# Loading V as rows of two neighbouring keys, between columns of ones

## The chip, the cores and the metric

The kernel runs on one core of one Trainium2 chip. TensorE multiplies matrices, VectorE, ScalarE and GpSimd compute elementwise, and 16 DMA engines move data; SyncE only issues transfers. The metric is the device time of one execution in microseconds (us); the number given for a kernel is the median of several executions. A profile is taken of one execution more, and it has its own time.

## The reference

The reference is one block of a conditioned transformer: an attention part with cached keys and values, then a mixer with two small matrix products and a feed-forward pair. Cut to the attention, where the change lies:

```
q = (h @ wq) as 32 heads of 128 columns            # h: [2048, 640], layer norm of x, modulated by c
scores = q @ k_cache.T * 128 ** -0.5               # per head [2048 queries, 2048 keys]
p = softmax(scores)
o = p @ v_cache                                    # v_cache: [32 heads, 2048 keys, 128], bf16
x = x + ga * (o of all heads, side by side, @ wo)
```

The sum over keys in the softmax's denominator and in `p @ v` does not depend on the order in which the keys are taken, as long as both factors of the product use the same one.

## The kernel before

**Steps and tiles.** The attention is one loop of 512 steps and some more at its end. Step `s` starts tile `s`: 128 queries of head `s // 16`, so that a head has 16 tiles. In one step, in the order in which each engine gets its work:

- TensorE makes the scores of tile `s` in two halves of 1024 keys into PSUM (`qk`, L294 with the helper L15), and behind each half the eight products of half a tile that is 8 steps older with V (`pv`, L307; `PVD = 8`). In most steps there is also one piece of the next head's queries (`q_piece`, L245) or of a transpose (`t_piece`, L261) behind each half.
- VectorE takes each half of the scores out of PSUM, multiplies by minus the scale, and keeps the smallest value of each row (L584). The result, `negS`, has three buffers.
- GpSimd takes the smaller of the two minima (L594, `nm`), and ScalarE makes the exponentials of the 2048 scores of each query with it as bias (L597): in `negS` float32, out `Pb` bf16, queries on the partitions, keys along the row.
- `pv` needs the exponentials with keys on the partitions. 14 of the 16 tiles of a head are transposed by DMA (`transpose`, L230), most of them two tiles at a time; tiles 3 and 10 of each head are transposed on TensorE (L261, copied out by L270 and L272). The transposed tile `PTs` has 16 blocks of 128 keys, which are the stationary operands of the 16 products of `pv`.
- ScalarE copies the finished outputs of two tiles out of PSUM (`Of`, L575). GpSimd makes the reciprocals of four tiles' sums at a time (`rcp`, L448, a power of minus one), multiplies each tile by it (`norm`, L455), and sends four tiles to a scratch array in HBM (L462).

**V and the sums.** `load_v` (L222) fills one of two buffers of `Vaug`: for each of the 16 blocks of 128 keys, partition `p` gets the 128 values of key `128 t + p`, that is one row of 256 B, and behind them lie two columns of ones that are written once (L350). Each product of `pv` reads 129 columns, 128 of V and a one, so that column 128 of the output is the sum of the exponentials.

**Order of the transfers.** All loads and all DMA transposes are issued by SyncE in one queue, in the order in which the program lists them; an issue that has to wait holds up those behind it. Counted by the tile `j` of a head's own steps, the queue has for each head: the transpose of tiles (0, 1), that of tile 2, the keys of the next head (L213, `j = 2`, itself a transposing load), tiles (4, 5), the weights of the queries of the head after next (L217, `j = 6`), tiles (6, 7), (8, 9), V of the next head (L222, `j = 9`), tile 11, tiles (12, 13), and (14, 15). A step's waits are worked out by a small planner (`Prog._add`): each operation names what it reads and writes, and gets a semaphore wait for every unfinished writer or reader of these.

**After the loop** the scratch array is read back transposed, multiplied by `wo`, and the mixer and the feed-forward part run (L532 to L846). The change does not touch these, but for the size of `Of`.

## Time and profile before

| | |
|---|---|
| median of 3 executions | 1593.01 us (1591.46 to 1596.07) |
| the profiled execution | 1592.4 us, of which the span from the first to the last instruction is 1590.6 us |
| granted TensorE clock, mean | 0.996 |
| VectorE, L584, half a tile of scores | 1024 of 1220 ns |
| ScalarE, L597, exponentials of a tile | 512 of 2018 ns |
| TensorE, L307, products with V | 8192 of 220 ns each from start to modelled end; they overlap |
| GpSimd, L448, reciprocals of four tiles | 128 of 1040 ns |
| DMA transposes of exponentials (L230) | 256, median 7.0 us from issue to landing |
| loads of V (L222) | 32 of 512 KB, median 5.0 us from issue to landing |

How to read it: each engine works through its own list, and an instruction that waits holds up the ones behind it. The profile gives, for each group of instructions of a source line, the busy time and the idle time of the engine just before them, with what ended that idle time. The rows of SPq are SyncE's own instructions. Instructions of one engine overlap by some tens of nanoseconds, so the step from one start to the next is shorter than a duration: L584 takes 1.22 us and follows itself after 1.145 us (641.26 and 642.41 us are two successive starts), L597 takes 2.0 us and holds ScalarE for 1.90 us (611.49 to 613.40 us, starts of two with nothing between). The loop takes the time from about 39 us to about 1280 us.

### The profile page before, as it was taken

Reading aid. Unit: us, or ns where it says so; the run is one execution under the profiler, and the core shown is the slowest. Engines: PE = TensorE matmul, PEld = TensorE weight load, DVE = VectorE, ACT = ScalarE, POOL = GpSimd, SP = SyncE. Lnnn points to the kernel's source line nnn. Section 1 sums busy time; section 2 is a strip of 40 time slices with the busy share of each in tenths; the row PEclk is TensorE's granted clock in tenths of the full one; section 3 lists DMA queues with packets and bytes.
Section 4 is the critical chain, followed back from the end, with each engine's and each line's share of the span. In section 5 each row is a group of like instructions: output and inputs, shape, how many; then the busy total and the mean of one; then the engine's idle time right before and its main releaser. Section 6 shows DMA issues by size and latency. Waiting matters only on the chain.

```text
span 1590.6 us, 33595 instructions
## 1 busy us (share of the span) xinstructions
PE 1477.4 (93%) x13976; PEld 916.9 (58%) x13207; DVE 1395.0 (88%) x2463; ACT 1295.8 (81%) x1145; POOL 622.0 (39%) x1396
## 2 busy tenths in 40 slices
PE   5899999999999999999999999999999889999999
PEld 3466655656565556665556565565656655555555
DVE  6999999999999999999999999999999646666435
ACT  4999999999999999999999999999999700036330
POOL 0244444444444444444444444444444523223100
PEclk9999999999999999999999999999999999999999
DMA  9999999999999999999999999999999997503000
GB/s 300 236 235 237 240 236 239 242 233 251 235 245 236 233 242 241 239 244 228 245 238 236 236 248 230 243 242 237 243 230 236 240 248 135 127 1 112 9 26 34
DMA packets 1167900, 333.53 MB, mean 210 GB/s; under 512 B 1148352, under 2 KB 1161728, under 8 KB 1167744
## 3 DMA queue, kind: packets, MB, share of 16 engines
q1 hardware_dynamic: 1161600, 314.59, 98.5%
q0 software_dynamic: 6144, 16.79, 3.7%
q8 instruction: 108, 1.77, 0.5%
q14 instruction: 48, 0.39, 0.1%
HBM read 43.48 MB, written 19.40 MB: 40 GB/s over the span
## 4 chain that ended last, share of the span: by engine, by line
DVE 34%; ACT 22%; PE 21%; DMA 13%; issue 9%; POOL 2%; SPq 0%; POOLq 0%; DVEq 0%
DVE negS L584 31%; ACT ring L597 18%; DMA ring<-ring 12%; PE Sps L532 8%; PE Sps L836 4%; ACT ring L270 2%; PE Oaug L787 2%; PE QPp L787 2%; PE Sps L772 1%; ACT kv L252 1%; ACT Of L575 1%; PE PTp L307 1%; DVE ring L272 1%; DMA negS<-o_scratch 1%; POOL small L594 1%
## 5 line engine op out<-in xcount | busy, mean ns | idle before, releaser
L584 DVE TENSOR_SCALAR_CACHE_REDUCE negS<-Sps 128x1024 f32<-128x1024 f32 x1024 | 1178.6, 1220 | 30.9 <-PE Sps L15 30.5
L597 ACT ACTIVATE ring<-negS,small 128x2048 bf16<-128x2048 f32 x512 | 1029.6, 2018 | 22.8 <-POOL small L594 20.7
L307 PEld LDWEIGHTS PTp<-kv,ring 128*128 128x128 bf16 x8192 | 550.7, 98 | 382.7 <-issue 112.9
L307 PE MATMUL PTp<-kv,ring 128*128 128x129 bf16 x8192 | 645.7, 220 | 49.0 <-DMA ring<-ring 48.6
L15 PE MATMUL Sps<-kv 128*128 128x512 bf16 x1024 | 387.9, 379 | 12.6 <-DVE negS L584 6.6
L594 POOL TENSOR_SCALAR small<-small 128x1 f32<-128x1 f32 x512 | 145.8, 285 | 631.5 <-DVE negS L584 631.5
L294 PE MATMUL Sps<-kv 128*128 128x512 bf16 x926 | 355.3, 384 | 21.9 <-DVE negS L584 10.8
L455 POOL TENSOR_SCALAR On<-Of,small 128x128 bf16<-128x128 f32 x512 | 190.0, 371 | 13.0
L294 PEld LDWEIGHTS Sps<-kv 128*128 128x128 bf16 x1024 | 98.3, 96 | 109.3 <-DVE negS L584 87.2
L448 POOL TENSOR_TENSOR small<-Of,small 128x4 f32<-128x4 f32 x128 | 133.1, 1040 | 9.2 <-ACT Of L575 9.2
L675 ACT COPY kv<-PTp 128x640 bf16<-128x640 bf16 x32 | 22.0, 692 | 127.7 <-PE PTp L672 127.6
L462 POOL DMA_DIRECT2D o_scratch<-On x128 | 103.1, 806 | 40.8 <-POOL On L455 37.2
L575 ACT COPY Of<-PTp 128x259 f32<-128x259 f32 x256 | 96.0, 375 | 14.3 <-PE PTp L307 14.3
L245 PE MATMUL Oaug<-hTx,kv 128*128 128x512 bf16 x264 | 100.4, 385 | 3.4 <-DVE hTx L404 3.4
L245 PE MATMUL QPp<-hTx,kv 128*128 128x512 bf16 x259 | 97.5, 381 | 2.4 <-ACT hTx L399 1.7
L584 DVE DVE_READ_ACCUMULATOR negS<-Sps 128x1 f32 x1024 | 84.9, 83 | 0.0
L631 POOL TENSOR_SCALAR negS<-negS 128x1 f32<-128x1 f32 x48 | 24.7, 514 | 138.5 <-DVE negS L640 138.3
L532 PE MATMUL Sps<-wo,negS 128*128 128x128 bf16 (+1 forms) x503 | 71.4, 300 | 4.5 <-DMA negS<-o_scratch 4.1
L532 PE MATMUL Sps<-wo,hTx 128*128 128x512 bf16 (+1 forms) x502 | 69.3, 297 | 0.5
L645 DVE TENSOR_TENSOR ring<-Sps,mod_bc 128x640 f32<-128x640 f32 x16 | 13.2, 825 | 62.1 <-PE Sps L532 40.7
L270 ACT COPY ring<-Oaug 128x1024 bf16<-128x1024 bf16 x64 | 65.4, 1022 | 0.0
L840 DVE TENSOR_TENSOR ring<-Sps,ring 128x640 f32<-128x640 f32 x15 | 12.4, 824 | 58.5 <-PE Sps L836 58.5
(91 smaller groups left out, 1043.4 us busy)
## 6 DMA issues: line engine op xcount, KB each, us to landing
kv<-in_A_v_cache_dram SPq DMA_DIRECT2D x32, 512.0 KB, 5.0
o_scratch<-On POOLq DMA_DIRECT2D x128, 128.0 KB, 3.8
kv<-in_A_wq_dram SPq DMA_DIRECT2D x32, 160.0 KB, 3.3
wo<-in_A_wo_dram SPq DMA_DIRECT2D x1, 5120.0 KB, 17.2
ring<-ring SPq DMA_TRANSPOSE x256, 7.0
ring<-in_A_x_dram SPq DMA_DIRECT2D x5, 640.0 KB, 7.0
ring<-in_w_mod_dram SPq DMA_DIRECT2D x1, 3200.0 KB, 13.3
out_dram<-wo SPq DMA_DIRECT2D x15, 160.0 KB, 1.8
```

Of the source, the lines that this page charges most:

```text
L15: return t.add_instruction(mybir.InstMatmult(name=t.bass.get_next_instruction_name(), ins=[t.lower_ap(rhs), t.lower_ap(lhsT)], outs=[t.low ...
L245: G.op("tensor", lambda t: t.matmul(JB[jb], wq[:, hb, q, :], hT[:, q, cc * 512:(cc + 1) * 512], start=(q == 0), stop=(q == KT - 1)), r=[(" ...
L294: ins = (t.matmul if c2 == 0 else partial(same_weights, t))(Sps[:, col:col + 512], QT[:, hb, j * 128:(j + 1) * 128], KTs[:, hb, col:col + ...
L307: ins = t.matmul(ob[:, 0:129], PTs[:, b, kt, :], Vaug[:, hb, kt, 0:129], start=(kt == 0), stop=(kt == NKT - 1))
L448: G.op("gpsimd", lambda g: g.tensor_tensor(out=rl[:, 4 * b:4 * b + 4], in0=Of[:].rearrange("p a z d -> p (a z) d")[:, 4 * b:4 * b + 4, 128 ...
L455: G.op("gpsimd", lambda g: g.tensor_scalar(out=On[:, b, z, :], in0=Of[:, 2 * b + z // 2, z % 2, 0:128], scalar1=rl[:, 4 * b + z:4 * b + z ...
L462: G.dma("gpsimd", lambda e: e.dma_start(o_scr[jj // 2:jj // 2 + 2, :, hh].rearrange("a p z d -> p a (z d)"), On[:, b].rearrange("p (a z) d ...
L532: ins = t.matmul(YB[b][:, c0:c0 + cw], OTj[pr % 2][:, 2 * hh + z, :], wo[:, hh, c0:c0 + cw], start=(hh == 0), stop=(hh == H - 1))
L575: G.op("scalar", lambda a, p=p: a.copy(Of[:, p % 4].rearrange("p z d -> p (z d)")[:, 0:259], PO[:, (p % 2) * 512:(p % 2) * 512 + 259]), r= ...
L584: G.op("vector", lambda v, half=half, s=s, r8=r8: v.tensor_scalar(out=negS[:, s % 3, half * 1024:(half + 1) * 1024], in0=Sps[:, half * 102 ...
L594: G.op("gpsimd", lambda g, r8=r8: g.tensor_scalar(out=nm[:, r8:r8 + 1], in0=nm0[:, r8:r8 + 1], scalar1=nm1[:, r8:r8 + 1], scalar2=None, op ...
L597: G.op("scalar", lambda a, s=s, r8=r8: a.activation(Pb[:, s % RP, :], negS[:, s % 3, :], ACT.Exp, bias=nm[:, r8:r8 + 1], scale=-1.0), r=[( ...
```

## The change

V is read in rows of two keys. In block `m` of 256 keys, partition `p` gets keys `256 m + 2 p` and the one behind it: one row of 512 B of HBM, put side by side. The buffer `Vblk` has eight such blocks per head, each 264 elements long: eight ones, the 128 values of the even key, the 128 of the odd key. The next block's ones follow directly.

A product of `pv` now reads 130 columns: two ones and the 128 values of an even key, or the 128 values of an odd key and the two ones that follow. The output is 132 columns wide (`OW`): columns 0 and 1 collect the sums over even keys, 2 to 129 the output, 130 and 131 the sums over odd keys. Even products write columns 0 to 129, odd ones 2 to 131. The first product of a tile has to start all 132 columns, so it reads a separate row of 132 columns, `Vfirst`: two ones, the even keys' values of the head's block 0, two zeros. `first_v` fills it by a GpSimd copy, once per head, in the step before the head's first `pv`.

Each tile's sum is the sum of columns 0 and 131, so `rcp` has one GpSimd addition more, ahead of the power. L575 copies 264 columns and no longer 259.

So that the transposed exponentials have the same order of keys, L597 reads the scores with a step of two: from a row of 2048 in the order block, key pair, even or odd, it reads block, even or odd, key pair, and writes the 2048 values one behind the other. The DMA transposes, their number and their place in the queue stay as they are, as do the places of all loads.

```diff
@@ -162,25 +162,30 @@
+                VS = 264
+                VB = NKT // 2 * VS
+                VL = 2 * VB + 8 + 24
+                OW = 132
...
-                kv = sb1("kv", [128, 2 * SK + 2 * NKT * 130 + 2 * KT * 128 + 2 * SQ], BF16)
-                small = sb1("small", [128, 4 * NQT + 32], F32)
+                kv = sb1("kv", [128, 2 * SK + VL + 2 * KT * 128 + 2 * SQ], BF16)
                 hTx = sb1("hTx", [128, US], BF16)
-                Of = sb1("Of", [128, 4, 2, 130], F32)
+                Of = sb1("Of", [128, 4, 2, OW], F32)
                 On = sb1("On", [128, 2, 4, 128], BF16)
+                small = sb1("small", [128, 4 * NQT + 50], F32)
...
+                Vfirst = small[:, 16:16 + OW // 2].bitcast(BF16)
...
-                Vaug = kv[:, o1:o2].rearrange("p (b k d) -> p b k d", b=2, k=NKT)
+                Vblk = kv[:, o1:o1 + 2 * VB].rearrange("p (b m z) -> p b m z", b=2, z=VS)
@@ -219,7 +224,8 @@
                 def load_v(h):
                     hb = h % 2
-                    G.dma("sync", lambda e: e.dma_start(Vaug[:, hb, :, 0:128], A_v_cache[0, h].rearrange("(t p) d -> p t d", p=128)),
+                    G.dma("sync", lambda e: e.dma_start(
+                        Vblk[:, hb, :, 8:264], A_v_cache[0, h].rearrange("(m p e) d -> p m (e d)", p=128, e=2)),
                           ("v", hb), w=[("V", hb)])
@@ -300,14 +306,25 @@
                 def pv(g, half):
                     hb = (g // NQT) % 2
                     b = g % RP
-                    ob = PO[:, ((g // 2) % 2) * 512 + (g % 2) * 130:]
+                    ob = PO[:, ((g // 2) % 2) * 512 + (g % 2) * OW:]
 
                     def f(t):
                         for kt in range(half * 8, half * 8 + 8):
-                            ins = t.matmul(ob[:, 0:129], PTs[:, b, kt, :], Vaug[:, hb, kt, 0:129],
+                            z = kt % 2
+                            v0 = o1 + hb * VB + (kt // 2) * VS + 6 + z * 130
+                            o0, rows = (0, Vfirst) if kt == 0 else (2 * z, kv[:, v0:v0 + 130])
+                            ins = t.matmul(ob[:, o0:o0 + (OW if kt == 0 else 130)], PTs[:, b, kt, :], rows,
                                            start=(kt == 0), stop=(kt == NKT - 1))
                         return ins
-                    G.op("tensor", f, r=[("PT", b, half), ("V", hb), "ones"], w=[("O", (g // 2) % 2)])
+                    G.op("tensor", f, r=[("PT", b, half), ("V", hb), "ones0", "ones", "vfz"] + (["vf"] if half == 0 else []), w=[("O", (g // 2) % 2)])
+
+                def first_v(h):
+                    hb = h % 2
+                    if h == 0:
+                        G.op("gpsimd", lambda g: g.memset(Vfirst, 0.0), w=["vfz0"] + MVK)
+                        G.op("gpsimd", lambda g: g.memset(Vfirst[:, 0:2], 1.0), r=["vfz0"], w=["vfz"])
+                    G.op("gpsimd", lambda g: g.tensor_copy(Vfirst[:, 2:130], Vblk[:, hb, 0, 8:136]), r=[("V", hb), "vfz"], w=["vf"])
+                MVK = [(n, i) for n, c in (("mv", NQT), ("sd", NQC), ("rstd", NQC)) for i in range(c)]
 
                 ringk = lambda a, b: [k for i in range(a // SK, -(-b // SK)) for k in (
                     [("Pb", i)] if i < RP else [("PT", i - RP, 0), ("PT", i - RP, 1)])]
@@ -347,7 +364,8 @@
                 G.op("gpsimd", lambda g: g.affine_select(out=ident[:], in_=ident[:], pattern=[[-1, 128]],
                                                          compare_op=ALU.not_equal, fill=1.0, base=0, channel_multiplier=1),
                      r=["id0"], w=["ident"])
-                G.op("gpsimd", lambda g: g.memset(Vaug[:, :, :, 128:130], 1.0), w=["ones"])
+                G.op("gpsimd", lambda g: g.memset(Vblk[:, :, :, 0:8], 1.0), w=["ones0"])
+                G.op("gpsimd", lambda g: g.memset(kv[:, o1 + 2 * VB:o1 + 2 * VB + 8], 1.0), w=["ones"])
                 G.op("scalar", lambda a: a.activation(s_col, c_sb, ACT.Silu), r=["c"], w=["scol"])
                 G.op("scalar", lambda a: a.activation(c_f, c_sb, ACT.Silu), r=["c"], w=["cf"])
                 for k in range(KT):
...
+                rsum = small[:, 8:16]
@@ -445,15 +464,18 @@
 
                 def rcp(gr):
                     b = gr % 2
+                    Og = Of[:].rearrange("p a z d -> p (a z) d")[:, 4 * b:4 * b + 4]
                     G.op("gpsimd", lambda g: g.tensor_tensor(
-                        out=rl[:, 4 * b:4 * b + 4], in0=Of[:].rearrange("p a z d -> p (a z) d")[:, 4 * b:4 * b + 4, 128],
-                        in1=mone, op=ALU.pow),
-                         r=[("Of", 2 * b), ("Of", 2 * b + 1), "mone"], w=[("rl", b)])
+                        out=rsum[:, 4 * b:4 * b + 4], in0=Og[:, :, 0], in1=Og[:, :, OW - 1], op=ALU.add),
+                         r=[("Of", 2 * b), ("Of", 2 * b + 1), "mone"], w=[("rsum", b)])
+                    G.op("gpsimd", lambda g: g.tensor_tensor(
+                        out=rl[:, 4 * b:4 * b + 4], in0=rsum[:, 4 * b:4 * b + 4], in1=mone, op=ALU.pow),
+                         r=[("rsum", b), "mone"], w=[("rl", b)])
 
                 def norm(gr, z):
                     b = gr % 2
                     G.op("gpsimd", lambda g: g.tensor_scalar(
-                        out=On[:, b, z, :], in0=Of[:, 2 * b + z // 2, z % 2, 0:128],
+                        out=On[:, b, z, :], in0=Of[:, 2 * b + z // 2, z % 2, 2:130],
                         scalar1=rl[:, 4 * b + z:4 * b + z + 1], scalar2=1.0, op0=ALU.mult, op1=ALU.mult),
                         r=[("Of", 2 * b + z // 2), ("rl", b)], w=[("On", b, z)])
                     if z < 3:
@@ -557,6 +579,8 @@
                             b1 = a_pe(1, None, (0,))
                         if 0 <= g_ < NG:
                             pv(g_, half)
+                        if half == 0 and 0 <= g_ + 1 < NG and (g_ + 1) % NQT == 0:
+                            first_v((g_ + 1) // NQT)
                         if s == 0 and half == 1:
                             q_head0(NQC - 1)
                         if h + 1 < H and 2 * j + half in QPIECE:
@@ -573,7 +597,7 @@
                     if 0 <= g_ < NG and g_ % 2 == 1:
                         p = g_ // 2
                         G.op("scalar", lambda a, p=p: a.copy(
-                            Of[:, p % 4].rearrange("p z d -> p (z d)")[:, 0:259], PO[:, (p % 2) * 512:(p % 2) * 512 + 259]),
+                            Of[:, p % 4].rearrange("p z d -> p (z d)"), PO[:, (p % 2) * 512:(p % 2) * 512 + 2 * OW]),
                             r=[("O", p % 2)], w=[("Of", p % 4)])
                     for fn, x, y in evacs:
                         if fn is q_evac or not by_dve(x, y):
@@ -595,7 +619,8 @@
                             out=nm[:, r8:r8 + 1], in0=nm0[:, r8:r8 + 1], scalar1=nm1[:, r8:r8 + 1], scalar2=None, op0=ALU.min),
                             r=[("nmh", 0, r8), ("nmh", 1, r8)], w=[("nm", r8)])
                         G.op("scalar", lambda a, s=s, r8=r8: a.activation(
-                            Pb[:, s % RP, :], negS[:, s % 3, :], ACT.Exp, bias=nm[:, r8:r8 + 1], scale=-1.0),
+                            Pb[:, s % RP, :].rearrange("q (m e p) -> q m e p", e=2, p=128),
+                            negS[:, s % 3, :].rearrange("q (m p e) -> q m e p", e=2, p=128), ACT.Exp, bias=nm[:, r8:r8 + 1], scale=-1.0),
                             r=[("negS", s % 3), ("nm", r8)], w=[("Pb", s % RP)])
                         if not is_pe(s):
                             if s % 2 == 1 and not is_pe(s - 1):
```

## The prediction

> **What bounds the kernel now.** I read the page first: busy times, the slices of DMA, then the chain that ended last.
>
> ```profile
> span 1590.6 us, 33595 instructions
> PE 1477.4 (93%) x13976; PEld 916.9 (58%) x13207; DVE 1395.0 (88%) x2463; ACT 1295.8 (81%) x1145; POOL 622.0 (39%) x1396
> DMA  9999999999999999999999999999999997503000
> DVE 34%; ACT 22%; PE 21%; DMA 13%; issue 9%; POOL 2%; SPq 0%; POOLq 0%; DVEq 0%
> ```
>
> No engine stands out, and DMA is at 9 in every slice of the loop. So I took the loop's middle alone, as one window (engine busy times PE, PEld, DVE, ACT, POOL, then clock, DMA share, GB/s), and the waits in it:
>
> ```profile
> 200.00:1200.00 1000.00, 933.51 (x9545) 596.89 (x8885) 976.66 (x1699) 981.54 (x811) 456.18 (x1046) 1.00 1.21 239
> PEld PTp L307 <- DMA ring<-ring: 90.4, 92, 2.4
> PE PTp L307 <- DMA ring<-ring: 44.3, 63, 1.9
> DVE negS L584 <- PE Sps L15: 23.1, 41, 1.6
> ```
>
> VectorE and ScalarE are both near 98%, and what keeps VectorE from 100% are 41 waits for the second half of the scores, which stand on TensorE behind a product with V that waits for a DMA transpose. The timelines show one such chain, at 642 us (SyncE's queue first, then TensorE and VectorE):
>
> ```profile
> 606.39 0.58 SPq L222 DMA_DIRECT2D kv<-in_A_v_cache_dram  x1
> 607.02 20.46 SPq L230 DMA_TRANSPOSE ring<-ring  x5
> 627.52 2.43 SPq L213 DMA_TRANSPOSE kv<-in_A_k_cache_dram  x1
> 629.99 4.49 SPq L230 DMA_TRANSPOSE ring<-ring  x1
> 634.52 0.58 SPq L217 DMA_DIRECT2D kv<-in_A_wq_dram  x1
> 635.15 9.22 SPq L230 DMA_TRANSPOSE ring<-ring  x2
> 644.42 0.58 SPq L222 DMA_DIRECT2D kv<-in_A_v_cache_dram  x1
> ...
> 642.86 0.64 PE L307 MATMUL PTp<-kv,ring 128*128 128x129 bf16 x8 [0.85 <-DMA ring<-ring]
> ...
> 644.20 1.22 DVE L584 TENSOR_SCALAR_CACHE_REDUCE negS<-Sps 128x1024 f32<-128x1024 f32 x1 [0.56 <-PE Sps L15]
> ```
>
> The queue has no gap: from one V load to the next (38.03 us) SyncE goes from issue to issue, and over 200 to 1200 us its issues fill 987 us. I followed each transpose of heads 2 to 29 through the trace: SyncE begins to issue it on average 4.0 us after its exponentials ended (never under 1.8), it lands 10.8 us after them, and of 168 pairs half are read by TensorE within 0.05 us of landing. The queue of transfers is therefore late by as much as the schedule allows, and the loop runs at its pace: a head takes 38.19 us (mean from exponential to exponential, heads 2 to 29), where heads 1 and 2 took 37.22 and 37.26. That is about VectorE's own need: 32 halves at 1.145 us and one L272 at 0.60 make 37.2. ScalarE needs 16 x 1.90 + 8 x 0.26 (L575) + 4 x 0.47 (L252) + 3 x 0.90 (L270) = 37.1. So a head can lose at most 0.97 us before VectorE is the bound; over the 28 heads that is 27 us.
>
> **The change part by part.** The profiled execution (1592.4 us, span 1590.6) lies 0.6 us under the median of 1593.0; the sum is made on the former and 0.6 is added.
>
> *The V load* (L222): 2048 packets of 256 B become 1024 of 512 B. The rate of packets of 256 B is in a stretch of pure transposes, 601 to 603 us, that of 1280 B in the loads of x, 12.5 to 13.5 us; the third line is a stretch with a V load, 684.4 to 687.4 us:
>
> ```profile
> DMA packets 2268, 0.58 MB, mean 290 GB/s; under 512 B 2268, under 2 KB 2268, under 8 KB 2268
> ...
> DMA packets 326, 0.40 MB, mean 398 GB/s; under 512 B 15, under 2 KB 326, under 8 KB 326
> ...
> DMA packets 2570, 0.65 MB, mean 218 GB/s; under 512 B 2570, under 2 KB 2570, under 8 KB 2570
> ```
>
> An engine gives off a packet of 256 B each 16 x 2000 / 2268 = 14.1 ns and one of 1280 B each 16 x 1000 / 311 = 51.4 ns (311 is 326 less the 15 small ones). On the line between them 512 B take 23.4 ns. A V load has 128 packets per engine now, 1.81 us, and then 64, 1.50 us: 0.31 us less at the least. What it costs in the queue now: from landing to landing, V with tile 11 takes 4.83 us, a single tile without V (tile 2) 2.24, so V takes 2.59. The 0.78 above 1.81 is the slow stretch in the third line. If the whole went with the number of packets, 1.30 would be saved. I take 0.5: the 0.31 and half of the 0.39 that the slow part would lose at best, since the trace does not tell whether that part goes with packets or with bytes. All of it lies on the queue, so on the path: 28 x 0.5 = 14.0 us less; bounds 28 x 0.31 = 8.7 and, held by VectorE, 27.
>
> The Trainium skill, DMA: Bandwidth & Descriptors, section "Why small descriptors are slow (HBM only)", gives a packet a fixed 3 cycles: 11 cycles for 256 B, so 19 for 512 B; as an estimate at its 850 MHz the 64 pairs of an engine save 64 x 3 = 192 cycles, 0.23 us a load, and the gain would be 6 us and not 14. Its 11 cycles would be 12.9 ns, where the trace has 14.1.
>
> *The exponentials* (L597) read with a step of two in 16 pieces. Nothing in the trace reads so. Low end: no change; a gain is excluded, for the same 2048 elements pass and a step from start to start of 1.90 us is 0.93 ns an element now. A row with pieces is L675, 640 elements written in five: 692 ns, where the medians of L252 (512, 566) and L270 (1024, 1019) give 679 by a straight line; 13 ns for four more pieces, 49 for 15. High end: each element costs two, 1.7 us more. I take zero: the 13 ns stem from the writing side. With 49 ns ScalarE needs 0.8 us more a head, 37.9, is the bound instead of the queue (37.7), and the gain is 0.3 x 28 = 8 us.
>
> The Trainium skill, Advanced Engine Details and Errata, section "Memory Cachelines", says of SBUF that two accesses to the same 16-byte line suffice for full speed; steps of two in float32 make exactly two. By that the sum stays at 14; no run here shows it yet.
>
> *Products with V* (L307): 18 columns more per tile (fifteen by 1, the first by 3). L294 to L15 step 0.22 us for 512 columns, 0.42 ns a column: 7.6 ns a tile, 3.9 us in all. They hide: a half with its extra piece takes TensorE 1.11 to 1.14 us (L307 to L307 at 632.69, 633.84, 634.98), where VectorE needs 1.145. Without this cover 3.9 us.
>
> *L575*: 5 columns more at 0.88 ns (the line above), 1.1 us in 256 copies, on ScalarE, which has 1.1 us a head to spare (0.6 after the change). Without cover 1.1 us.
>
> *The addition before the power*, 128 times on GpSimd: at least 0.28 us (L594, one element), at most 1.04 (L448, same form). I take 0.4 by L594, and 0.1 between the two. In a step with a reciprocal GpSimd was idle 0.50 us before the next L594 at 605.37, which is just filled. At 1.04 this L594 would come 0.6 us late, behind which only ScalarE's next exponential waits; that one started 0.87 us after L594 ended (606.54 against 605.67). Uncovered it would be at most 128 x 0.6 = 77 us.
>
> *first_v*: 32 copies of 128 elements, 0.37 us each by L455. It waits for the product that reads the old row last in the step, and L594 stands behind it; but that L594 waits for the second half of the scores, which TensorE makes after that product and VectorE reads for 1.2 us more. The head's first product comes a step later, so the copy is done. Uncovered 12 us. The memsets are one or two more of about 0.1 us (L431) before the loop, where GpSimd is idle. The stores to the scratch array (L462) come behind the addition by two steps and more. SyncE's queue keeps all its issues and places; the V load has one new reader to wait for, the old copy of first_v, done a head earlier.
>
> Sum: 1592.4 - 14.0 = 1578.4, and 0.6 for the median: 1579.0.
>
> **The rivals.**
>
> *The whole cover is used.* The load shrinks by 1 us or more, and VectorE becomes the bound at 37.2 us a head: 1593 - 27 = 1566. For it: the slow stretch looks like a start with few bytes under way. Against: that stretch has 99 GB/s in its worst slice but up to 276 in its middle, near the 290 of full rate, and there only the 0.31 is to be had.
>
> *Only the packets' own time.* If the slow start and end of a V load stay as long, a load saves 0.31 us, 8.7 in all: 1584. For it: they may be the wait for HBM's first bytes, which a transfer has once whatever its packets. Against: the rate climbs over a whole microsecond, as if few packets were let out at a time. (The page's fixed cost per packet would stand here, with 1587.)
>
> *Nothing arrives.* A transpose behind V pauses, for example no packets from 611.7 to 612.0 and hardly any to 612.8, while tile 11's has begun; if such pauses are set by the issue and not by V's packets, the time saved turns into a longer pause: 1593. Against: SyncE's issue of a pair takes 4.2 to 5.3 us, about its packets' 3.6, so the issue follows the drain.
>
> *Slower: the stepped read holds ScalarE.* From (38.19 - 37.1) / 16 = 68 ns more per exponential on (3.4%), ScalarE needs more than the queue does now; from 78 ns on the kernel is slower by over 0.3%. At 200 ns, a tenth, a head takes 40.3 us: 32 x 2.1 = 67 more, 1660; at the high end 2.5 ms. For it: no row with such a read exists. Against: L675's small price.
>
> **How the numbers follow.** 0.3% (4.8 us) is about what a measurement can tell from no change. The forecast has 0.40, only the packets' time 0.13, the whole cover 0.10; the likeliest's own range is 1568 to 1588, from a load that saves 0.9 us to one that saves 0.31 with TensorE's 3.9 us uncovered, and the 49 ns case lies in it. Nothing arrives, 1588 to 1598, has 0.15; slower 0.22, half of it beyond 1605. Faster 0.63, same 0.15, slower 0.22. Range 1563 (VectorE's bound, a little over) to 1605, which leaves out 0.11 above and next to nothing below.
>
> **What would show it.** The page: 32768 fewer packets. L597 at 2.02 us: the stepped read is free; at 2.09 or more it isn't. The waits of L307 for DMA and of VectorE for L15 fall to about half; a head at 37.7 us. From landing to landing V with tile 11 at 4.3 us. A new wait of ScalarE for L594, far over the 15 us of the window 200 to 1200, would show the addition uncovered. Wrong would make it: L597 longer by 70 ns, or SyncE's gapless queue as it was with a shorter V load.

## The result and the profile after

The changed kernel takes 1636.29 us (median of 5 executions, 1636.14 to 1640.62), the kernel before 1594.94 us beside it (median of 5, 1591.46 to 1599.06). The ratio is 1.0274, with a 95% interval of 1.0258 to 1.029: slower by 2.7%, where 1579.0 us and 0.9% faster had been predicted. The profiled execution of the changed kernel has a span of 1638.5 us, 47.9 us more than that of before; the granted clock is 0.996 in both.

The line numbers move by the edit. Exponentials are L621 now (L597 before), VectorE's scores L608 (L584), products with V L316 (L307), transposes L236 (L230), the V load L227 (L222), the copy of finished outputs L599 (L575), the addition and the power L468 and L471 (L448), and `nm` L618 (L594).

The page of the changed kernel, its span, its busy times, its packets, its chain by engine, two rows of its groups (busy us, mean ns of one, idle time before) and the row of V's loads (KB each, us from issue to landing):

```profile
span 1638.5 us, 34045 instructions
...
PE 1510.6 (92%) x14231; PEld 920.0 (56%) x13207; DVE 1413.6 (86%) x2463; ACT 1365.3 (83%) x1145; POOL 660.1 (40%) x1559
...
DMA packets 1135133, 333.54 MB, mean 204 GB/s; under 512 B 1082816, under 2 KB 1128960, under 8 KB 1134976
...
ACT 77%; PE 19%; DVE 3%; DMA 1%; issue 0%; POOL 0%; SPq 0%; POOLq 0%
...
L621 ACT ACTIVATE ring<-negS,small 128x2048 bf16<-128x2048 f32 x512 | 1251.1, 3312 | 2.1 <-POOL small L618 1.9
L608 DVE TENSOR_SCALAR_CACHE_REDUCE negS<-Sps 128x1024 f32<-128x1024 f32 x1024 | 1196.2, 1222 | 58.1 <-ACT ring L621 45.3
...
kv<-in_A_v_cache_dram SPq DMA_DIRECT2D x32, 512.0 KB, 5.2
```

The change did what it says: the page before had 1167900 packets, now there are 32767 fewer. But of the chain, which was spread over VectorE, ScalarE, TensorE and the transfers, 77% is ScalarE's now. The exponentials hardly wait any more (2.1 us in all), and VectorE's largest wait is for the exponentials, which free `negS`. A V load takes 5.2 us from issue to landing, where it took 5.0.

The loop's middle as one window (engine busy times PE, PEld, DVE, ACT, POOL, then clock, DMA share, GB/s) and the waits in it:

```profile
200.00:1200.00 1000.00, 924.56 (x9371) 579.38 (x8562) 957.29 (x1640) 1000.00 (x783) 468.80 (x1135) 1.00 1.17 231
```

```profile
PEld Sps L300 <- DVE negS L608: 126.5, 416, 1.2
...
DVE negS L608 <- ACT ring L621: 38.8, 70, 0.9
...
PEld PTp L316 <- DMA ring<-ring: 4.3, 9, 1.0
...
PE PTp L316 <- DMA ring<-ring: 0.7, 2, 0.5
```

ScalarE is busy for all of the 1000 us (981.54 before). The waits of the products for a DMA transpose, 90.4 and 44.3 us before, are 4.3 and 0.7 us here. SyncE begins to issue a transpose 0.69 us after its exponentials ended on average (4.0 before), and a pair is read 1.67 us after it landed (median; 0.05 before). So the queue of transfers is no longer late: it waits for ScalarE.

What one exponential costs is read from starts. Two rows of ScalarE's timeline before, then a stretch of it now, and pieces of the chain now:

```profile
611.49 3.92 ACT L597 ACTIVATE ring<-negS,small 128x2048 bf16<-128x2048 f32 x2
615.29 0.39 ACT L575 COPY Of<-PTp 128x259 f32<-128x259 f32 x1
```

```profile
612.36 3.40 ACT L621 ACTIVATE ring<-negS,small 128x2048 bf16<-128x2048 f32 x1
614.42 1.62 ACT L599 COPY Of<-PTp 128x264 f32<-128x264 f32 x1
614.68 5.44 ACT L621 ACTIVATE ring<-negS,small 128x2048 bf16<-128x2048 f32 x2
618.81 1.58 ACT L599 COPY Of<-PTp 128x264 f32<-128x264 f32 x1
```

```profile
598.72 2.06 ACT ring L621
600.79 0.27 ACT Of L599
601.05 2.08 ACT ring L621
603.14 0.47 ACT kv L258
603.61 2.04 ACT ring L621
```

The row's mean of 3.31 us is not the price: the instruction behind an exponential starts 2.06 us after it (612.36 to 614.42), and two exponentials with nothing between them hold ScalarE 4.13 us (614.68 to 618.81), where two held it 3.80 us before (611.49 to 615.29). The recorded durations overlap by some 1.3 us here, those of the copies behind an exponential too (1.62 us where 0.38 was recorded before, though the copy holds ScalarE 0.26 us as before). From start to the next start an exponential takes 2.06 us (median over the loop), where it took 1.905: 0.15 us or 8% more, 0.075 ns an element.

A head needs of ScalarE 37.1 + 16 x 0.15 = 39.5 us, and heads 2 to 29 take 39.64 on average (38.19 before). These 28 heads give 28 x 1.44 = 40.4 of the 47.9 us. Of the rest, 2.4 us lie in head 1, which had run at VectorE's 37.2 us before, 1.3 us each in heads 0 and 30, and 2.2 us between the start of head 31 and the end.

### The profile page after: what moved, and what is told of

The parts are those of the page before. It is cut to its first block, busy times and chain, and to the rows that moved or that the text cites. A ratio compares the mean times of both kernels' runs of the same rounds, so it can differ in the third digit from the quotient of the medians.

```text
span 1638.5 us, 34045 instructions
## 1 busy us (share of the span) xinstructions
PE 1510.6 (92%) x14231; PEld 920.0 (56%) x13207; DVE 1413.6 (86%) x2463; ACT 1365.3 (83%) x1145; POOL 660.1 (40%) x1559
## 4 chain that ended last, share of the span: by engine, by line
ACT 77%; PE 19%; DVE 3%; DMA 1%; issue 0%; POOL 0%; SPq 0%; POOLq 0%
ACT ring L621 63%; PE Sps L554 8%; ACT ring L276 5%; ACT Of L599 4%; ACT kv L258 4%; PE Sps L861 3%; PE Oaug L812 2%; PE QPp L812 2%; PE Sps L797 1%; DMA negS<-o_scratch 1%; DVE negS L608 1%; DVE ring L390 1%; PE Oaug L732 1%; PE QPp L732 1%; PE PTp L697 1%; DVE ring L402 0%
## 5 line engine op out<-in xcount | busy, mean ns | idle before, releaser
L621 ACT ACTIVATE ring<-negS,small 128x2048 bf16<-128x2048 f32 x512 | 1251.1, 3312 | 2.1 <-POOL small L618 1.9
L608 DVE TENSOR_SCALAR_CACHE_REDUCE negS<-Sps 128x1024 f32<-128x1024 f32 x1024 | 1196.2, 1222 | 58.1 <-ACT ring L621 45.3
L316 PEld LDWEIGHTS PTp<-kv,ring 128*128 128x128 bf16 x7680 | 504.0, 97 | 207.4 <-issue 53.1
L316 PE MATMUL PTp<-kv,ring 128*128 128x130 bf16 x7680 | 606.9, 220 | 0.0
L599 ACT COPY Of<-PTp 128x264 f32<-128x264 f32 x256 | 390.3, 1525 | 12.5 <-PE PTp L316 12.5
L618 POOL TENSOR_SCALAR small<-small 128x1 f32<-128x1 f32 x512 | 147.5, 288 | 618.7 <-DVE negS L608 618.6
L15 PE MATMUL Sps<-kv 128*128 128x512 bf16 x1024 | 388.0, 379 | 0.0
L276 ACT COPY ring<-Oaug 128x1024 bf16<-128x1024 bf16 x64 | 138.5, 2164 | 0.0
L471 POOL TENSOR_TENSOR small<-small 128x4 f32<-128x4 f32 x128 | 133.6, 1044 | 10.0
L484 POOL DMA_DIRECT2D o_scratch<-On x128 | 103.5, 809 | 40.8 <-POOL On L477 37.2
L316 PE MATMUL PTp<-small,ring 128*128 128x132 bf16 x512 | 113.2, 221 | 3.0 <-ACT Of L599 2.1
L258 ACT CAST kv<-QPp 128x512 bf16<-128x512 f32 x64 | 108.1, 1688 | 1.6 <-PE QPp L251 1.6
L258 ACT CAST kv<-Oaug 128x512 bf16<-128x512 f32 x64 | 107.2, 1675 | 1.7 <-PE Oaug L251 1.7
L316 PEld LDWEIGHTS PTp<-small,ring 128*128 128x128 bf16 x512 | 50.0, 98 | 85.8 <-issue 27.8
L608 DVE DVE_READ_ACCUMULATOR negS<-Sps 128x1 f32 x1024 | 85.3, 83 | 0.0
```

What stands on the lines that cost most here:

```text
L15: return t.add_instruction(mybir.InstMatmult(name=t.bass.get_next_instruction_name(), ins=[t.lower_ap(rhs), t.lower_ap(lhsT)], outs=[t.low ...
L258: G.op("scalar", lambda a: a.copy(QT[:, hb, cc * 512:(cc + 1) * 512], JB[jb]), r=[("J", jb)], w=[("QT", hb, cc)])
L276: G.op("scalar", lambda a: a.copy(dst, src), r=[("J", jb)], w=[("PT", g % RP, r)])
L316: ins = t.matmul(ob[:, o0:o0 + (OW if kt == 0 else 130)], PTs[:, b, kt, :], rows, start=(kt == 0), stop=(kt == NKT - 1))
L471: G.op("gpsimd", lambda g: g.tensor_tensor(out=rl[:, 4 * b:4 * b + 4], in0=rsum[:, 4 * b:4 * b + 4], in1=mone, op=ALU.pow), r=[("rsum", b) ...
L599: G.op("scalar", lambda a, p=p: a.copy(Of[:, p % 4].rearrange("p z d -> p (z d)"), PO[:, (p % 2) * 512:(p % 2) * 512 + 2 * OW]), r=[("O", ...
```

## The experiments

Ratios are to executions of the kernel before on the same chip beside them, with 95% intervals; the medians of before lie between 1592.82 and 1593.34 us. "Landing to landing" is the mean over heads 2 to 29 of the time from the landing of tiles (8, 9) to that of tile 11, between which V is loaded. It differs from head to head; the standard error of such a mean is 0.13 to 0.27 us.

### Which part of the change costs the time

**plain_exp**, the changed kernel with the exponentials read as before:

```
-  Pb[...].rearrange("q (m e p) -> q m e p", e=2, p=128), negS[...].rearrange("q (m p e) -> q m e p", e=2, p=128), ACT.Exp, ...
+  Pb[:, s % RP, :], negS[:, s % 3, :], ACT.Exp, ...
```

> The changed kernel with the exponentials read as before, one behind the other; all else of the change stays (exponentials of one key then meet V of another, so the output is another one, the work the same). Theory A, the stepped read alone makes the kernel slower (an exponential held ScalarE 1.905 us from start to start before, 2.055 after): the exponential is back at 1.905, and what the V load itself is worth shows, 1579 by the prediction's step, a head at 37.7 us. Rival B, the V load gives nothing: 1593. Rival C, the addition on GpSimd, the wider products or the wider copy hold the loop too: above 1598.

It took 1590.3 us, ratio 0.9998 (0.998 to 1.0016). From start to start an exponential takes 1.906 us again.

**step_only**, the kernel before with the stepped exponentials and nothing else of the change:

```
-  Pb[:, s % RP, :], negS[:, s % 3, :], ACT.Exp, ...
+  Pb[...].rearrange("q (m e p) -> q m e p", e=2, p=128), negS[...].rearrange("q (m p e) -> q m e p", e=2, p=128), ACT.Exp, ...
```

> The kernel before with the exponentials read with the step of two in 16 pieces and nothing else (V stays in its old order, so the products pair other keys). Theory A: 2.055 us from exponential to exponential, ScalarE full at 37.1 + 16 x 0.15 = 39.5 us a head, 1593 + 31 x 1.4 = 1636, the changed kernel's time. Rival C (other parts of the change hold it): under 1620.

It took 1638.07 us, ratio 1.0283 (1.0266 to 1.0301). So the stepped read alone makes the whole loss, and all the rest of the change together, V's longer rows among it, changes nothing that could be measured. The window 200 to 1200 us and a wait in it, of plain_exp:

```profile
200.00:1200.00 1000.00, 929.48 (x9527) 593.88 (x8867) 974.44 (x1697) 980.36 (x810) 481.93 (x1174) 1.00 1.18 238
```

```profile
PEld PTp L316 <- DMA ring<-ring: 83.2, 84, 3.0
```

That is the kernel before again: ScalarE at 980 of 1000 us, the products waiting 83.2 us for transposes (90.4 before), a head of 38.32 us. From landing to landing V with tile 11 takes 4.95 us, where it took 4.83.

**two_pieces**, the changed kernel with the same step of two, but in 2 pieces of 1024 instead of 16 of 128; the products take V's blocks in the order that matches:

```
+  Pb[...].rearrange("q (e j) -> q e j", e=2), negS[...].rearrange("q (j e) -> q e j", e=2), ACT.Exp, ...
...
-  z = kt % 2;  v0 = ... (kt // 2) * VS ...
+  z = kt // 8; v0 = ... (kt % 8) * VS ...
```

> The changed kernel with all even keys of the 2048 ahead of all odd ones: the exponential reads with a step of two as before the edit, but in 2 pieces of 1024 in place of 16 of 128; the products take V's blocks in that order. If the price is one of the pieces (150 ns / 15 = 10 ns each): 1.915 us, and the time that the plain read gives, 1579. If it is one of the step (150 ns / 2048 = 0.073 ns an element): 2.055 us and 1636.

It took 1636.91 us, ratio 1.028 (1.0265 to 1.0295), with ScalarE again busy for 1000 of 1000 us and 2.06 us from start to start. Eight times fewer pieces change nothing: the price is the step's, not the pieces'.

**step_no_v**, the changed kernel without V's loads from head 2 on:

```
-  if j == PVD + 1 and h + 1 < H:
+  if j == PVD + 1 and h + 1 < 2:
```

> The changed kernel without the loads of V from head 2 on (old values are multiplied, so the output differs). If ScalarE alone sets the pace of the changed kernel: 1633 to 1638 us, no gain from a queue that is 30 us shorter. If V's loads still cost something beside it: under 1630 us.

1638.22 us, ratio 1.0279 (1.0262 to 1.0296). Taking 512 KB a head out of the queue is worth nothing in the changed kernel: ScalarE alone sets its pace.

**step_four**, the kernel before with a step of four elements:

```
+  Pb[...].rearrange("q (m e p) -> q m e p", e=4, p=128), negS[...].rearrange("q (m p e) -> q m e p", e=4, p=128), ACT.Exp, ...
```

> The kernel before with the exponentials reading the scores with a step of four elements (16 B) instead of one, and no other edit; the keys are then paired wrongly with V, so the output differs. If the price goes by the bytes that lie between two elements read: about 3 times 0.15 us, 2.35 us from start to start, 16 x 0.45 - 1.1 = 6.1 us a head and 1593 + 195 = 1790 us. If it is one price for leaving the row's order: 2.055 us and 1637 us again. If only the second read of a 16-byte piece were cheap: some figure between 2.1 and 3 us, and 1650 to 2100 us.

2557.36 us, ratio 1.6047 (1.6017 to 1.6077), beyond all three expectations. Pieces of its chain:

```profile
602.68 3.84 ACT ring L597
606.52 0.47 ACT kv L252
607.00 3.86 ACT ring L597
610.85 0.27 ACT Of L575
```

From start to start 3.86 us: the price is not in proportion to the step (0.15 us for 8 B, 1.95 for 16 B). With one element read in each 16 bytes the exponentials take twice as long, with two nearly as long as with four. No run has a step of three, so where between 8 and 16 B the price jumps is open.

**k_step**, the changed kernel with plain exponentials, but TensorE reads the keys' columns with a step of two (4 B in bf16), so that the scores come out with the even keys first; the products with V take its blocks as in two_pieces (not shown again):

```
-  KTs[:, hb, col:col + 512]
+  KTs[:, hb].rearrange("p (j e) -> p e j", e=2)[:, half, c2 * 512:c2 * 512 + 512]
```

> The changed kernel with the step moved from ScalarE to TensorE: the score products read the keys' columns with a step of two (bf16, so 4 bytes), even keys in the first half, odd in the second; the exponentials read one behind the other. If TensorE reads so without loss, L15 stays at 379 ns and the time is that of the plain exponentials, 1579 by the prediction's step. Rival: a product of 512 columns takes twice as long, 0.43 us, TensorE needs 0.85 us more a step, 1593 + 512 x 0.6 = 1900.

1591.98 us, ratio 0.9994 (0.998 to 1.0009). The second product of a half takes 387 ns (L15, 379 before), and from start to start the two products of a half take 463 ns, where they take 441 in plain_exp (medians). VectorE covers that, so the order of keys that the longer rows ask for is nearly free on TensorE; the longer rows still bring nothing. From landing to landing V with tile 11 takes 5.14 us.

### What the V load costs, and why its longer rows saved nothing

**no_v_load**, the kernel before without V's loads from head 2 on (the same edit as in step_no_v):

> The kernel before without the V loads of heads 2 to 31 (the two buffers keep heads 0 and 1; the rest of the work is the same). Theory Q, the queue of transfers sets the pace and a V load takes 2.6 us of it: a head falls from 38.2 us to VectorE's 37.2, 1593 - 27 = 1566. Rival H, V is hidden anyway (what paces the loop is not the queue, or not at V's place): 1593.

1563.32 us, ratio 0.9809 (0.9793 to 0.9824). The window and the only row of waits of the products for a transpose in it:

```profile
200.00:1200.00 1000.00, 976.92 (x9993) 632.66 (x9132) 999.76 (x1746) 999.19 (x832) 471.01 (x1076) 1.00 1.18 231
```

```profile
PEld PTp L307 <- DMA ring<-ring: 1.0, 3, 0.6
```

The queue did set the pace before, and V's load was worth 30 us there; with it gone, VectorE (999.76) and ScalarE (999.19) are full at once.

**half_v**, the kernel before with only the first 8 of V's 16 blocks loaded from head 2 on:

```
+  nt = NKT if h < 2 else NKT // 2
-  Vaug[:, hb, :, 0:128], A_v_cache[0, h]...
+  Vaug[:, hb, 0:nt, 0:128], A_v_cache[0, h, 0:nt * 128]...
```

> The kernel before, but from head 2 on only the first half of V is loaded (8 of 16 blocks of 128 keys, 256 KB; the rest of the buffer keeps an older head's values, so the output differs). Full loads gave 1593 us, none at all 1563. If V costs the queue by its bytes or packets: 1593 - 15 = 1578 us, V with tile 11 at about 3.5 us from landing to landing. If it costs its start: 1587 to 1593 us and over 4.2 us. If the cost is taken up wholly by TensorE's and VectorE's own needs below half a load: under 1570 us.

1573.28 us, ratio 0.9874 (0.9857 to 0.9891). V with tile 11 takes 3.57 us from landing to landing; it is 4.83 with the whole V and 1.97 with none. A head takes 37.70 us, and in the window VectorE is at 988.84. So half of the bytes, which is half of the packets too, takes about half of the place in the queue; there is no large fixed part. Whether bytes or packets set it, the next two runs ask.

**wide_rows**, plain_exp with one row of 4096 B for each partition, 16 keys, in a buffer whose ones it overwrites (the lines that write the ones are left out here):

```
-  Vblk[:, hb, :, 8:264], A_v_cache[0, h].rearrange("(m p e) d -> p m (e d)", p=128, e=2)
+  kv[:, o1 + hb * VB + 8:o1 + hb * VB + 8 + 16 * 128], A_v_cache[0, h].rearrange("(p e) d -> p (e d)", p=128)
```

> The changed kernel with plain exponentials and V read in one row of 16 keys (4096 B) per partition, 128 packets a load in place of 1024 (other keys meet the exponentials and the ones are overwritten, so the output is another one). If V's place in the queue goes with packets at all, the load takes 8 x 159 ns = 1.3 us and a start, and the time falls below that of 512 B, to 1580. If the start (the wait for HBM) or the bytes set it, V with tile 11 stays at 4.8 to 5.0 us and the time at 1590 to 1593.

1596.45 us, ratio 1.0016 (1.0002 to 1.0029); landing to landing 5.36 us. An eighth of the packets saves nothing.

**v_128**, the kernel before with V in two transfers of 64 columns each, 4096 rows of 128 B:

```
+  for c in range(2):
+      ... Vaug[:, hb, :, c * 64:c * 64 + 64], A_v_cache[0, h, :, c * 64:c * 64 + 64].rearrange("(t p) d -> p t d", p=128)
...
```

> The kernel before with V loaded in two transfers, the first 64 columns and then the last 64: 4096 rows of 128 B instead of 2048 of 256 B, the same bytes and the same place in the queue. If V's place goes by bytes alone: V with tile 11 at 4.8 to 5.2 us from landing to landing and 1590 to 1600 us. If it goes by packets below some size: 6.6 us and more, 1593 + 30 x 1.8 = 1647 us.

1612.96 us, ratio 1.012 (1.0098 to 1.0142); landing to landing 6.37 us, 1.54 more than with rows of 256 B, of which the transposes behind it make good a part, for a head is 0.82 us longer (39.01). Rows of 128 B cost more than rows of 256 B; rows of 512 and of 4096 B save nothing. (Two transfers are also two starts; v_split below finds no price of a second start.) The figures together, all of heads 2 to 29:

| V's rows | bytes a head | landing to landing, V with tile 11 |
|---|---|---|
| none | 0 | 1.97 us |
| 256 B, half | 256 KB | 3.57 us |
| 128 B | 512 KB | 6.37 us |
| 256 B (before) | 512 KB | 4.83 us |
| 512 B (plain_exp) | 512 KB | 4.95 us |
| 512 B (k_step) | 512 KB | 5.14 us |
| 4096 B | 512 KB | 5.36 us |

How a load of the same bytes in half the packets comes to the same time is seen in the rate of all 16 engines around it, from the traces, as the mean of 27 V loads in GB/s, in tenths of a us, every third of them shown, before V's landing:

```
us before landing   3.65 3.35 3.05 2.75 2.45 2.15 1.85 1.55 1.25 0.95 0.65 0.35
256 B (before)       191  186  196  239  260  260  258  227  204  160  104   49
512 B (plain_exp)    204  137   85   98  126  220  291  315  305  269  185   89
```

Rows of 512 B do move faster once they flow, 315 GB/s against 260. But at the start, where the engines go over from transposes to V, the rate falls to some 85 to 125 GB/s for about 0.9 us, nearly all of it rows of 512 B already. The kernel before doesn't fall below 182 there, and that takes back what is won. The other two kernels with longer rows have the same low stretch (k_step down to 89 GB/s, wide_rows to 73). Why the start is slower with longer rows is not shown by these runs.

**v_split**, the kernel before with V in two halves of 256 KB, the second behind tiles (12, 13):

```
   if j == PVD + 1 and h + 1 < H:
-      load_v(h + 1)
+      load_v(h + 1, (0,))
+  if j == 13 and h + 1 < H:
+      load_v(h + 1, (1,))
...
```

> The kernel before with the load of V in two halves of 256 KB (8 blocks of 128 keys each), the first where it was, behind tiles (8, 9), the second behind tiles (12, 13). If V's place goes by bytes: no change, 1589 to 1597 us, half a load in each place (V with tile 11 at 3.6 us). If each load has a slow start of its own, some 0.8 us: 1593 + 30 x 0.8 = 1617 us. If smaller bursts help the transposes behind them: under 1588 us.

1594.72 us, ratio 1.0005 (0.999 to 1.002); V's first half with tile 11 takes 3.65 us, and tiles (14, 15), behind the second half, land 5.77 us after tiles (12, 13), where it was 4.42. Twice as many starts cost nothing that could be measured; a load's place can be divided.

### Three ways to get the queue's time back

**v_pool** and **v_act**, the kernel before with V's loads from head 1 on issued by GpSimd and by ScalarE instead of SyncE:

```
-  G.dma("sync", lambda e: e.dma_start(Vaug[:, hb, :, 0:128], ...
+  G.dma("gpsimd" if h >= 1 else "sync", lambda e: e.dma_start(Vaug[:, hb, :, 0:128], ...
```

```
-  G.dma("sync", lambda e: e.dma_start(Vaug[:, hb, :, 0:128], ...
+  G.dma("scalar" if h >= 1 else "sync", lambda e: e.dma_start(Vaug[:, hb, :, 0:128], ...
```

> The kernel before with V of heads 1 to 31 issued by GpSimd at the same place of the program, rows of 256 B as before: its packets no longer stand between transposes in SyncE's queue, so the engines can work on a transpose while V waits for HBM. Theory Q with an exposed start of V: most of what leaving V out gives, about 1570 (a head 37.4). If V's bytes are what costs: 0.51 MB at 290 GB/s, 1.8 of 2.6 us, stay, and the gain is 28 x 0.8 = 22 at most, 1571 or above. Against: GpSimd's issue (the stores of 128 KB take it 0.81 us) may hold up the minimum of the next tile; rival 1593 or above.

> The kernel before with the loads of V from head 1 on issued by ScalarE in its own queue instead of by SyncE. If V's packets fill the pauses of the transposes: towards 1563 us, that of no load at all, plus what the issue takes of ScalarE (0.6 us a head of 1.1 spare). If they take the transposes' place on the 16 engines as before: 1590 to 1600. If they hold a transpose up for several us, as they did when GpSimd issued them: 1640 us and more.

v_pool took 1664.01 us (its four executions scatter from 1641.8 to 1697.66, so no ratio is given), v_act 1631.04 us, ratio 1.0245 (1.0222 to 1.0268). The longest waits of the products and of VectorE in the window 200 to 1200 us, first of v_pool, then of v_act, and v_act's row of V's loads (KB each, us from issue to landing):

```profile
PEld PTp L307 <- DMA ring<-ring: 92.8, 26, 11.2
DVE negS L584 <- PE Sps L15: 91.4, 30, 11.5
```

```profile
PEld PTp L307 <- DMA ring<-ring: 64.8, 32, 4.9
...
PE PTp L307 <- DMA ring<-ring: 49.1, 26, 4.4
```

```profile
kv<-in_A_v_cache_dram ACTq DMA_DIRECT2D x31, 512.0 KB, 8.7
```

Waits are fewer than before, but up to 11.2 and 4.9 us long, where the longest was 2.4: a transpose beside V's packets is held up, and the products with it. From issue to landing a transpose of heads 2 to 29 takes up to 20.1 us in v_pool and 13.4 in v_act, 9.0 before. It is not the bytes: in one such stretch of v_pool, 636 to 640 us, all 16 engines move 0.20 MB together, 50 GB/s, while a transpose that was issued at 625.73 us lands at 643.13. What holds them up is not shown. In v_act the weights with their pair take 8.58 us from landing to landing (5.39 before), since V's packets come there. **k_step_v_pool** is k_step with V's loads from head 1 on issued by GpSimd, by the same edit as v_pool:

> The kernel with V in rows of two keys, TensorE reading the keys' columns with the step and plain exponentials, and V issued by GpSimd for heads 1 to 31. As the one with rows of 256 B from GpSimd, 1570; if GpSimd's part of the issue goes with the number of rows (1024 in place of 2048), some microseconds under it.

1650.82 us (1634.2 to 1664.59), ratio 1.032 (1.0261 to 1.0379). The longer rows do not mend it.

**wq_four**, the kernel before with the queries' weights loaded for four heads at a time, in rows of 1024 B instead of 256 B; they lie in the place of the last eight heads of `wo`, which are loaded in the last head:

```
-  if j == 6 and h + 2 < H:
-      load_wq(h + 2)
+  if j == 6 and h % 4 == 1 and h + 3 < H:
+      load_wq(h + 3, h + 7)
...
+  if h + 1 == H and j == 12:
+      G.dma("sync", ... wo[:, WH:H] ...)
```

> The kernel before, but the weights of the queries are loaded for four heads at a time in rows of 1024 B instead of for each head in rows of 256 B; they lie in the place of the last eight heads of wo, which are loaded in the last head. Theory (the queue of transfers sets the pace, and a load costs it mostly its start): in the kernel before the weights cost the queue about 1.07 us a head (5.39 us from landing to landing with the pair behind them, 4.32 without), three of four starts go, about 0.8 us x 28 = 22 us less, some 4 us back for the late part of wo: 1575 us, and not under 1563, where VectorE is full. Rival (what a load gives free is taken by a longer pause of the transposes behind it, as it seemed with V's wider rows): 1590 to 1596.

1608.66 us, ratio 1.0086 (1.0065 to 1.0107): slower than either expectation. Of the seven heads with a load for four, four take 41.5 to 42.6 us, two 39.1 and 39.3, and the first 37.2; the others of heads 2 to 29 take 37.2 to 39.3, 37.85 on average. Four loads in one place have the bytes of four, and come at once: the products' longest wait is 4.4 us. The heads between win 0.34 us each on average and cannot win more than about 1, since VectorE holds them at 37.2.

No version that computes everything was measurably faster than the kernel before.

## Why the prediction was wrong

The forecast was 0.9% faster; the rival "slower: the stepped read holds ScalarE" is what happened.

- **The step that failed first: "the exponentials ... I take zero".** Measured: 0.15 us for each, between the ends that the prediction had (0 and 1.7), on ScalarE, the place that the rival named. (The upper end is 1.90 by the prediction's own 0.93 ns an element, and its 2.5 ms goes with 1.90; with 1.7 it would be 2.43. The doubling came with a step of four: 1.95 us, 2557 us.) Its point, 68 ns, is passed, and its own sum with 150 ns instead of 200 gives a head of 39.5 us and 1593 + 32 x 1.3 = 1635; measured 1636.29. The mechanism was laid out and only the term was mis-sized, but it decided the sign. The evidence for zero was the row of L675, which has pieces and no step; two_pieces shows that pieces were not the question. No row of before had a stepped float32 read, and with 68 ns (3.4%) between gain and loss the forecast stood on an unpriced term.
- **The rule of the Trainium skill**, Advanced Engine Details and Errata, "Memory Cachelines", reads "Need at least two hits on a cacheline to absorb SRAM access latency", and the prediction took two as enough for full speed. The knee is in the right place by these runs: 2.06 us with two elements to a line of 16 bytes, 3.86 with one. But two are not full speed: they are 8% off here (1.905 us with four), and on an engine with 1.1 us a head to spare that is the whole result.
- **The second step that failed: "I take 0.5" for V's load**, with 0.31 as the least. Measured in plain_exp: nothing (4.95 us from landing to landing against 4.83, 1590.3 us against 1592.82). The 0.31 came from a line between packets of 256 B in pure transposes and of 1280 B in other loads, as if an engine's time per packet were the load's time. It isn't: the flow is faster and the start slower, and with rows of 256 B and more V's place does not shrink with fewer packets. No run has the longer rows without the wider products, so a small gain under a small loss isn't excluded by the time alone; the landings speak against it. So without the stepped read the rival "nothing arrives" would have been right, in its time. The fixed 3 cycles a packet of the Trainium skill (DMA: Bandwidth & Descriptors, "Why small descriptors are slow (HBM only)"), an estimated 0.23 us a load in the prediction, do not show from 256 to 512 B here either.
- **Right: what bounds the kernel before.** The queue of transfers set the pace, with 0.97 us a head to gain before VectorE is full. no_v_load took 1563.32 us where "the whole cover is used" had 1566, and half_v's head took the 37.70 us that the forecast had hoped for from longer rows.
- **Right: the rest costs nothing that shows.** plain_exp holds all of it, the products' 18 columns, the 5 columns of the copy (378 ns, 375 before), the addition, the copies for the first block, and is at 0.9998. (The starts of L307 that the prediction gives for TensorE's need are 1.15 and 1.14 us apart, VectorE's pace, and no measure of that need; the cover is there all the same.) The addition took 0.199 us in the changed kernel (L468), less than the 0.28 taken as the least; no wait of ScalarE for L618 came of it (23.0 us over the span of plain_exp against 20.7).
- **The line to watch.** "L597 at 2.09 or more" was the right line to watch, but its mean of 3.31 us would have been read as a price over eight times too high. The waits of the products for transposes fell as announced, by much more than half, and for another reason: the queue got time because ScalarE was late.

## What to carry to other kernels

Before an access pattern of an elementwise engine is changed to suit a transfer, work out how much that engine may lose before it is the bound; where the spare time is a few per cent, a pattern that no row of the trace shows must be priced by a run, or the reordering moved to an engine whose price is known (here TensorE's read of the keys, some 10 ns a product). A load's place in a full queue of transfers is not its packets' time: ask by leaving half of it out, which is one edit and tells a fixed start from what grows with the load; then change the rows' length at the same bytes, which tells packets from bytes. When a group's duration grows, take the price from start to start before believing the mean.

## What the runs showed of the hardware

- ScalarE's exponentials of 2048 float32 elements from SBUF hold it 1.905 us read in order, 2.06 with a step of 8 B (the same with 16 pieces and with 2), and 3.86 with a step of 16 B.
- With a step, the recorded duration (3.31 us) is some 1.3 us longer than the time until the next instruction starts, and that of short copies behind it grows too (0.38 to 1.53 us on average).
- TensorE's moving operand in bf16 read with a step of 4 B took 387 ns for 512 columns where it took 379 (two products from start to start 463 ns, 441 in order).
- A load of 512 KB between DMA transposes in one queue takes no smaller place with longer rows (landing to landing with the transpose behind it 4.83 us at 256 B, 4.95 and 5.14 at 512, 5.36 at 4096), a smaller one with half the load (3.57), and more with rows of 128 B (6.37).
- With the same load issued from another engine, TensorE waited up to 4.9 us (ScalarE's queue) and 11.2 us (GpSimd's) for a transpose, 2.4 before.
